# Moving one of four input tiles behind the first weight load, at the start of a fused state-space and dense-layer kernel

## Chip, cores, metric

The kernel runs on one core of a Trainium2 chip. The metric is device time in microseconds (us), median of several executions; lower is better. All times in profiles count from the start of the profiled execution (its span, about 1.4 us shorter than the device time of the same execution). PE is TensorE, PEld its weight loads, DVE is VectorE, ACT is ScalarE, SPq is the queue that issues most DMAs.

## The reference

```python
xn = _layernorm(x)                         # x: 1 x 2048 x 1024, bf16
h  = xn @ w1 + b1                          # w1: 1024 x 3584
dense = (h * tanh(softplus(h))) @ w2       # w2: 3584 x 1024
# state-space part: a diagonal complex recurrence over the 2048 rows of xn
out = x + ssm(xn) + dense
```

This is a condensed form of the reference: the state-space part (two complex projections around the recurrence) plays no role here.

## The kernel before

The kernel works on four blocks of 512 rows. A block is four x tiles of 128 rows (256 KB each). Only the head of the kernel matters here: the first block's x tiles must be loaded, normalized and transposed before TensorE can multiply them with w1. Weights stream through a ring of seven slots of 512 KB. All these loads are issued from one queue, SP, in the order of this code:

```python
    for h in range(2):                      # x tile 0, in two halves
        SP.dma(lambda e, h=h: e.dma_start(xx[:, 0, 0, h * 512:(h + 1) * 512], ...), ...)
    for q in range(1, NQ):                  # x tiles 1, 2, 3
        load_x(SP, 0, q)
    ...                                     # four small loads on the ACT queue
    for i in range(NRING):                  # weights: ring 0 ... ring 6
        ring_load()
        if i == 5:
            SP.dma(... dsk[:] <- A_Dskip.partition_broadcast(P) ...)
```

Who uses what, in program order (cut; `keep_busy(n)` are n dummy matmuls, "fillers", meant to bring TensorE to its faster pace; in the profile of the kernel before, the time from one to the next goes from 107 to 56 ns at about 5.5 us):

```python
    for q in range(2):                      # tiles 0 and 1: statistics on VectorE
        first_sums_v(q, 0); first_sums_v(q, 1); first_var_v(q); first_sqrt(q)
    ...
    first_apply(0);    first_transpose(0)   # normalize on VectorE, transpose on TensorE
    first_apply(1, 2); first_transpose(1)
    keep_busy(8)                            # the last 8 fillers
    first_mean_a(3)                         # tile 3: statistics on ScalarE
    first_copy(0, VE, 0, 4);  first_copy(1, VE, 0, 4)      # lower halves of xnT
    first_copy(0, AC, 4, NK); first_copy(1, AC, 4, NK)     # upper halves, on ScalarE
    ...
    first_sums_v(2, 0); first_sums_v(2, 1)  # tile 2: statistics on VectorE
    ...
    first_apply(2); first_apply(3)
    for f in range(4): first_half(f, 0, 0, NK // 2)        # 16 w1 matmuls: ring 0
    for f in range(4):
        first_half(f, 0, NK // 2, NK)                      # 16 w1 matmuls: ring 1
        if f in (2, 3): first_transpose(f); first_copy(f, VE)
```

So TensorE needs, in this order: tiles 0 and 1, ring 0, ring 1, tile 2, tile 3.

Of the kernel before, what the change touches and what calls it, by code (L numbers as in the profile page):

```python
# [135 lines left out]
def bass_parallel_sum__ssm_conv_s5__dense_activation_mish__prompt_kernel(  # L136
    nc: bass.Bass,
    A_x: bass.AP,
    A_Lambda_re: bass.AP,
    A_Lambda_im: bass.AP,  # L140
    A_B_re: bass.AP,
    A_B_im: bass.AP,
    A_C_re: bass.AP,
    A_C_im: bass.AP,
    A_log_dt: bass.AP,
    A_Dskip: bass.AP,
    B_x: bass.AP,
    B_w1: bass.AP,
    B_b1: bass.AP,
    B_w2: bass.AP,  # L150
    out: bass.AP,
):
    build_kernel(nc, A_x, A_Lambda_re, A_Lambda_im, A_B_re, A_B_im, A_C_re, A_C_im,
                 A_log_dt, A_Dskip, B_w1, B_b1, B_w2, out)


def build_kernel(nc, A_x, A_Lambda_re, A_Lambda_im, A_B_re, A_B_im, A_C_re, A_C_im,
# [7 lines left out]
    NQ = TB // P  # L165
# [13 lines left out]
    SP = Queue(nc, "sp")  # L179
# [104 lines left out]
    def load_x(queue, blk, q):  # L284
        r0 = blk * TB + q * P
        i = blk % 2
        queue.dma(lambda e: e.dma_start(xx[:, i, q, :], A_x[0, r0:r0 + P, :]),  # L287
                  s_xx[i][q] if blk else s_x0[q], writes=[b_xx[i][q]])

    for h in range(2):  # L290
        SP.dma(lambda e, h=h: e.dma_start(xx[:, 0, 0, h * 512:(h + 1) * 512], A_x[0, 0:P, h * 512:(h + 1) * 512]),  # L291
               DmaSem(nc, "d_x00_%d" % h), writes=[b_xx[0][0].parts[h]])
    for q in range(1, NQ):
        load_x(SP, 0, q)
    for src, r0, n in ((A_log_dt, 2 * NJ, NJ), (A_Lambda_im, NJ, NJ), (A_Lambda_re, 0, NJ),
                       (B_b1, 3 * NJ, NF)):
# [9 lines left out]
    def ring_load():  # L306
        i = n_loaded[0]
        if i >= len(items):
            return
        n_loaded[0] += 1  # L310
        kind, g = items[i]
        s = i % NRING
        if kind == "w1":

            dst = ring[:, s, :].rearrange("p (k f) -> p k f", k=NK // 2)
            r0 = (g % 2) * D // 2
            src = B_w1[r0:r0 + D // 2, (g // 2) * 512:(g // 2 + 1) * 512].rearrange("(k p) f -> p k f", p=P)
        else:
            dst = ring[:, s, :].rearrange("p (f d) -> p f d", f=2)
            src = B_w2[g * 256:(g + 1) * 256, :].rearrange("(f p) d -> p f d", p=P)  # L320
        SP.dma(lambda e: e.dma_start(dst, src), s_ring[s], writes=[b_ring[s]])

    for i in range(NRING):
        ring_load()
        if i == 5:
            SP.dma(lambda e: e.dma_start(dsk[:], A_Dskip.partition_broadcast(P)), s_dsk, writes=[b_dsk])

# [571 lines left out]
```

## Time and profile before

| kernel before | |
|---|---|
| median of the first 3 runs | 621.56 us (621.54 to 623.44) |
| span of the profiled execution | 620.4 us |
| TensorE busy | 99% of the span |
| first w1 matmul starts | 9.25 us |
| ring 0 landed | 9.20 us |

Lines of the page of the kernel before: the span; busy time and share of each engine; and the chain of work that ended last, as shares of the span by engine.

```profile
span 620.4 us, 7330 instructions
...
PE 613.6 (99%) x2905; PEld 287.3 (46%) x2961; DVE 462.2 (74%) x677; ACT 247.5 (40%) x161; POOL 50.6 (8%) x47
...
PE 98%; DMA 1%; issue 1%; SPq 0%; DVE 0%
```

TensorE is the limit for 98% of the time. The 1% of DMA is the head. The timeline of the issue queue (start, duration, queue, line, what is loaded, count):

```profile
0.79 0.88 SPq L291 DMA_DIRECT2D xx<-in_A_x_dram  x2
1.72 1.40 SPq L287 DMA_DIRECT2D xx<-in_A_x_dram  x3
3.16 6.28 SPq L321 DMA_DIRECT2D ring<-in_B_w_dram  x6
```

The DMA view of a window that holds only the issue of ring 0 (the last number is the time from issue to landing):

```profile
ring<-in_B_w_dram SPq DMA_DIRECT2D x1, 512.0 KB, 6.0
```

The chain of the first 30 us, in order of time (start, duration, what):

```profile
3.16 6.04 DMA ring<-in_B_w_dram
9.20 0.05 issue
9.25 3.23 PE ps L521 x28
```

Ring 0 is issued at 3.16, lands 6.04 us later, and the first w1 matmuls (line 521) follow at once. The timeline of the same stretch (in brackets: idle time before the group and what ended it):

```profile
8.33 0.61 PE L475 MATMUL ps<-filler 128*128 128x128 bf16 x8
8.74 1.41 DVE L349 BATCH_NORM_STATS2 stats<-xx 128x6 f32<-128x512 bf16 x2
9.24 2.95 PEld L521 LDWEIGHTS ps<-xnT,ring 128*128 128x128 bf16 x28 [0.48 <-DMA ring<-in_B_w_dram]
9.25 3.23 PE L521 MATMUL ps<-xnT,ring 128*128 128x256 bf16 x28 [0.31 <-DMA ring<-in_B_w_dram]
12.21 0.54 PEld L391 LDWEIGHTS ps<-ident,xn 128*128 128x128 bf16 x8
...
18.86 3.23 PEld L663 LDWEIGHTS ps<-xnT,ring 128*128 128x128 bf16 x16
```

The fillers end at 8.94 and TensorE idles 0.31 us for ring 0. VectorE takes tile 2's statistics at 8.74 without waiting. Tile 2's transposes follow at 12.21. The last line is the first weight load of the full-width matmuls, after which no wait of TensorE is listed; it serves below as the mark for the end of the head.

### The profile page before, as it was taken

Reading aid. Unit: us, or ns where it says so; the run is one execution under the profiler, and the core shown is the slowest. Engines: PE = TensorE matmul, PEld = TensorE weight load, DVE = VectorE, ACT = ScalarE, POOL = GpSimd, SP = SyncE. Lnnn points to the kernel's source line nnn. Section 1 sums busy time; section 2 is a strip of 40 time slices with the busy share of each in tenths; the row PEclk is TensorE's granted clock in tenths of the full one; section 3 lists DMA queues with packets and bytes.
Section 4 is the critical chain, followed back from the end, with each engine's and each line's share of the span. In section 5 each row is a group of like instructions: output and inputs, shape, how many; then the busy total and the mean of one; then the engine's idle time right before and its main releaser. Section 6 shows DMA issues by size and latency. Waiting matters only on the chain.

```text
span 620.4 us, 7330 instructions
## 1 busy us (share of the span) xinstructions
PE 613.6 (99%) x2905; PEld 287.3 (46%) x2961; DVE 462.2 (74%) x677; ACT 247.5 (40%) x161; POOL 50.6 (8%) x47
## 2 busy tenths in 40 slices
PE   8999999999999999999999999999999999999998
PEld 7544444444444444444444444444444444444444
DVE  6897899999467599998147759999624856999603
ACT  5689996440069940000008992000001999000000
POOL 1999000000100000000010000000000000000000
DMA  8999965840364300783054430276203541033001
GB/s 286 266 259 260 224 113 189 218 137 0 122 200 153 135 1 36 204 196 109 17 187 136 144 128 1 88 201 172 83 35 104 171 166 68 1 121 117 1 0 69
DMA packets 95804, 79.41 MB, mean 128 GB/s; under 512 B 48922, under 2 KB 78234, under 8 KB 95770
## 3 DMA queue, kind: packets, MB, share of 16 engines
q1 hardware_dynamic: 92272, 71.64, 41.1%
q10 hardware_dynamic: 2538, 4.14, 1.8%
q0 software_dynamic: 960, 3.15, 1.6%
q8 instruction: 24, 0.39, 0.3%
q14 instruction: 10, 0.08, 0.0%
HBM read 63.19 MB, written 4.19 MB: 109 GB/s over the span
## 4 chain that ended last, share of the span: by engine, by line
PE 98%; DMA 1%; issue 1%; SPq 0%; DVE 0%
PE ps L742 49%; PE ps L663 30%; PE ps L684 18%; PE ps L521 1%; DMA ring<-in_B_w_dram 1%; PE ps L756 0%; SPq L287 0%; PE ps L391 0%; SPq L291 0%; DVE xx L810 0%
## 5 line engine op out<-in xcount | busy, mean ns | idle before, releaser
L742 PE MATMUL ps<-ring,act 128*128 128x512 bf16 x880 | 193.2, 379 | 0.8
L663 PE MATMUL ps<-xnT,ring 128*128 128x512 bf16 x840 | 184.4, 379 | 0.8
L642 ACT ACTIVATE act<-hb 128x3584 bf16<-128x3584 bf16 x16 | 50.9, 3183 | 223.5 <-DVE hb L671 223.5
L742 PEld LDWEIGHTS ps<-ring,act 128*128 128x128 bf16 x896 | 87.7, 98 | 105.7
L663 PEld LDWEIGHTS ps<-xnT,ring 128*128 128x128 bf16 x856 | 83.8, 98 | 100.8
L671 DVE TENSOR_SCALAR hb<-ps,par 128x512 bf16<-128x512 f32 x112 | 82.4, 747 | 56.0 <-PE ps L663 54.8
L684 PE MATMUL ps<-xnT,BT 128*128 128x512 bf16 x500 | 110.5, 379 | 0.6
L742 PE MATMUL ps<-CT,hT 128*128 128x512 bf16 x494 | 109.2, 379 | 0.6
L689 DVE TENSOR_TENSOR mt<-ps,tab 128x1024 bf16<-128x1024 f32 x64 | 75.3, 1219 | 17.6 <-PE ps L684 16.6
L684 PEld LDWEIGHTS ps<-xnT,BT 128*128 128x128 bf16 x512 | 50.1, 98 | 60.4
L742 PEld LDWEIGHTS ps<-CT,hT 128*128 128x128 bf16 x506 | 49.5, 98 | 59.7
L707 DVE TENSOR_TENSOR_SCAN hT<-cs,qi,hT 128x512 bf16<-128x512 f32 x48 | 58.9, 1267 | 0.0
L787 DVE TENSOR_TENSOR xx<-ps,xx 128x1024 bf16<-128x1024 f32 (+1 forms) x16 | 18.8, 1189 | 46.1 <-PE ps L742 46.0
L643 ACT ACTIVATE act<-act 128x3584 bf16<-128x3584 bf16 x16 | 51.0, 3190 | 0.2
L644 ACT ACTIVATE act<-act 128x3584 bf16<-128x3584 bf16 x16 | 51.0, 3190 | 0.2
L712 DVE TENSOR_TENSOR mt<-hT,tab 128x1024 bf16<-128x1024 bf16 x64 | 41.4, 688 | 1.1
L649 DVE TENSOR_TENSOR act<-act,hb 128x3584 bf16<-128x3584 bf16 x16 | 32.3, 2016 | 1.3 <-ACT act L644 1.3
L287 POOL DMA_DIRECT2D xx<-in_A_x_dram x12 | 6.7, 559 | 253.2 <-DVE xx L787 247.4
L618 ACT ACTIVATE ct<-CT,cs 128x512 f32<-128x512 bf16 x16 | 11.5, 720 | 26.7 <-DVE CT L620 25.9
L643 ACT ACT_TABLE_LOAD x16 | 20.5, 1283 | 0.3
L644 ACT ACT_TABLE_LOAD x16 | 20.5, 1283 | 0.3
L707 DVE TENSOR_TENSOR_SCAN hT<-cs,hT 128x512 bf16<-128x512 f32 x16 | 18.7, 1208 | 0.0
(86 smaller groups left out, 276.5 us busy)
## 6 DMA issues: line engine op xcount, KB each, us to landing
ring<-in_B_w_dram SPq DMA_DIRECT2D x112, 512.0 KB, 3.9
out_dram<-xx ACTq DMA_DIRECT2D x15, 256.0 KB, 2.1
xx<-in_A_x_dram POOLq DMA_DIRECT2D x12, 256.0 KB, 3.8
xx<-in_A_x_dram SPq DMA_DIRECT2D x3, 256.0 KB, 3.5
xx<-in_A_x_dram SPq DMA_DIRECT2D x2, 128.0 KB, 2.3
dsk<-in_A_Dskip_dram SPq DMA_DIRECT2D x1, 256.0 KB, 8.0
xnT<-xn SPq DMA_TRANSPOSE x12, 4.5
BT<-in_A_B_re_dram SPq DMA_TRANSPOSE x8, 5.8
```

The costliest lines, as they stand in the source:

```text
L642: aop(lambda e: e.activation(a, hs, AF.Exp), reads=[b_hb[g % 2]], writes=[b_act[g]])
L643: aop(lambda e: e.activation(a, a, AF.Ln, bias=1.0), reads=[b_act[g]], writes=[b_act[g]])
L644: aop(lambda e: e.activation(a, a, AF.Tanh), reads=[b_act[g]], writes=[b_act[g]])
L649: vop(lambda e: e.tensor_tensor(a, a, hs, op=ALU.mult), reads=[b_act[g], b_hb[g % 2]], writes=[b_act[g]])
L663: PE.mm(lambda e, k=k, w=w: e.matmul(ps[:, bank, :], lhsT=w, rhs=xnT[:, k, :], start=k == 0, stop=k == NK - 1), reads=[b_ring[s]] + b_xnT, ...
L671: vop(lambda e: e.tensor_scalar(hb[:, hs, :], ps[:, bank, :], b1(f), None, op0=ALU.add), reads=[b_ps[bank], b_par], writes=[b_hbf[hs]])
L684: PE.mm(lambda e, j=j, ci=ci, k=k, bank=bank: e.matmul(ps[:, bank + ci, :], lhsT=BT[:, ci, j, k, :], rhs=xnT[:, k, :], start=k == 0, stop= ...
L689: vop(lambda e, s=s, u=u, j=j: e.tensor_tensor(mt[:, s, :, :], u, tab[:, s, j, :].unsqueeze(1).to_broadcast([P, 2, TB]), op=ALU.mult), rea ...
L707: vop(lambda e, ci=ci, init=init: e.tensor_tensor_scan(out=hT[:, ci, j, :], data0=cj("r", j).to_broadcast([P, TB]), data1=hT[:, ci, j, :], ...
L712: vop(lambda e, s=s: e.tensor_tensor(mt[:, s, :, :], hT[:, :, j, :], tab[:, s, j, :].unsqueeze(1).to_broadcast([P, 2, TB]), op=ALU.mult), ...
L742: PE.mm(lambda e: e.matmul(ps[:, u, :], lhsT=lhsT, rhs=rhs, start=st_, stop=last), reads=reads, writes=[b_ps[u]], first=st_, last=last)
L787: vop(lambda e: e.tensor_tensor(xr, src, xr, op=ALU.add), reads=b_ps[bank:bank + n] + [b_x], writes=[b_x])
```

## The change

The intent: load in the order of use. Tile 2 is wanted after the first weights, so it gives way to them.

```diff
-    for q in range(1, NQ):
+    for q in (1, 3):
         load_x(SP, 0, q)
 ...
     for i in range(NRING):
         ring_load()
+        if i == 0:
+            load_x(SP, 0, 2)
```

## The prediction

> **What bounds the kernel.** TensorE does. The page gives PE 613.6 of 620.4 us (99%), and the chain of waits puts 98% on PE. The waits by engine show no PE wait after 15 us. The change touches only the first 13 us. There PE waits 1.0 us for its first filler, then 0.3 us for a filler behind a VectorE reciprocal, and 0.31 us for the first weights: the fillers end at 8.94 us, the first w1 matmul starts at 9.25. Those 0.31 us, 0.05% of the time, are the whole target.
>
> **The loads before.** The timeline of the DMA-issuing queue: x tile 0 in halves at 0.79 and 1.25, tiles 1, 2, 3 at 1.72, 2.18, 2.67, first weights (ring 0, 512 KB) at 3.16, ring 1 at 3.63. Issue plus time to landing (DMA view of narrow windows): x2 5.7, x3 6.5, ring 0 9.2, ring 1 10.7, ring 2 12.2, ring 3 13.7. Rings land 1.5 us apart, 512 KB at about 350 GB/s: the DMA engines are the limit, not the issue. Landings in the trace come in sixteen parts: 15 of ring 0 by 8.45 us, the last at 9.20. This fits the Trainium skill, "DMA: Bandwidth & Descriptors", section "Queues, rings and completion order": each engine consumes descriptors in ring order, so here order of issue decides order of landing.
>
> **What the change moves.** Nothing is added or removed; x2 (256 KB) goes behind ring 0. At 1.5 us per 512 KB, that is worth 0.75 us (estimate):
> - x3 lands near 5.7 (was 6.5). ScalarE reads it at 6.82: no gain.
> - Ring 0 lands near 8.45 (was 9.20), before the fillers end (8.94); the VectorE copies of xnT end at 8.70. The first w1 matmul starts at about 8.95: up to 0.3 us saved.
> - Ring 1 and later ones have the same bytes ahead and stay at 10.7. PE needs ring 1 after 16 matmuls of 109 ns, 1.75 us: 8.95 + 1.75 = 10.70. The slack of 0.28 us is used up; some 0.05 us can return as a wait there.
> - x2 lands near 9.2 (was 5.7). VectorE took its statistics at 8.74: now about 9.25. Normalized tile 2 ends at 12.0 instead of 11.50, tile 3 at 12.7 instead of 12.23. PE transposed them at 12.21 and 13.09, now would at 11.95 and 12.85: about 0.05 us of wait on tile 2, none on tile 3.
> - Ring 3 (13.7) is wanted at about 13.85: no wait.
>
> So 0.31 us saved, 0.05 to 0.1 given back: net about 0.2 us (0.1 to 0.3), kept to the end since PE is continuous from there. Span 620.4 to about 620.2.
>
> **Predicted time:** 621.3 us, against 621.56. Eight times in ten between 620.3 and 622.3, mostly spread of runs (the three before lie 1.9 us apart). Faster by over 2%: 0.005; within 2%: 0.99; slower by over 2%: 0.005.
>
> **What would show it.** Timeline: first w1 matmul at 8.9 to 9.0, no wait on the ring before it; VectorE's statistics of x2 wait on DMA (about 0.4 us) and start near 9.25; ring 1 still lands near 10.7; the first full-width weight matmul (19.19 before) at about 19.0, everything after 0.2 us earlier.
>
> **What would make it wrong.** If x2 lands after 9.4, the transposes of tile 2 wait for it and the gain vanishes or becomes a loss of a few tenths; if the lagging engine of the sixteen doesn't lose the 0.75 us, ring 0 stays late and nothing is gained. Neither can reach 2%.

## The result

| | before | after |
|---|---|---|
| median, 6 runs each | 621.73 us (621.49 to 623.44) | 621.25 us (621.11 to 622.30) |
| ratio | | 0.999, 95% interval 0.9977 to 1.0003 |
| span of the profiled execution | 620.4 us | 620.0 us |

A ratio is the mean time of one kernel's fast runs over that of the other's of the same rounds, so it is not quite the ratio of the medians quoted. Where the granted clock is listed it is 1.0 for all but two: the slowest run of dsk_first2 (624.82 us) and the slowest of swap_only3 (623.72 us), both at 0.997 and both without a profile.

The page after. The two added lines of code shift all line numbers behind them by two, so L521 is L523 now, L663 is L665.

```profile
span 620.0 us, 7386 instructions
...
PE 616.7 (99%) x2961; PEld 287.2 (46%) x2961; DVE 462.4 (75%) x677; ACT 247.6 (40%) x161; POOL 50.6 (8%) x47
...
PE 99%; DVE 1%; DMA 0%; issue 0%; DVEq 0%
```

PE shows 56 more matmuls and 3.1 us more busy time, though both programs have the same matmuls: the trace before lacks 56 matmul records (2905, with 2961 weight loads). No conclusion may be drawn from that difference. In the chain, 1% has gone from DMA to DVE. The issue queue after:

```profile
1.72 0.92 SPq L287 DMA_DIRECT2D xx<-in_A_x_dram  x2
2.68 0.44 SPq L321 DMA_DIRECT2D ring<-in_B_w_dram  x1
3.16 0.50 SPq L287 DMA_DIRECT2D xx<-in_A_x_dram  x1
3.71 5.60 SPq L321 DMA_DIRECT2D ring<-in_B_w_dram  x5
```

The DMA view of the window with the issue of ring 0:

```profile
ring<-in_B_w_dram SPq DMA_DIRECT2D x1, 512.0 KB, 4.9
```

Issued at 2.68, landed 4.9 us later at 7.6, not at 9.2. The chain after, from its start:

```profile
0.79 2.23 DMA xx<-in_A_x_dram
...
8.38 0.45 PE ps L477 x8
8.82 3.24 PE ps L523 x28
```

Ring 0 is out of the chain: it now runs from the landing of x tile 0 through VectorE and the fillers (L477) into the first w1 matmuls. The timeline:

```profile
8.21 0.61 PE L477 MATMUL ps<-filler 128*128 128x128 bf16 x8
8.70 1.66 PEld L523 LDWEIGHTS ps<-xnT,ring 128*128 128x128 bf16 x16
8.73 3.33 PE L523 MATMUL ps<-xnT,ring 128*128 128x256 bf16 x28
9.05 1.42 DVE L351 BATCH_NORM_STATS2 stats<-xx 128x6 f32<-128x512 bf16 x2 [0.34 <-DMA xx<-in_A_x_dram]
10.57 1.21 PEld L523 LDWEIGHTS ps<-xnT,ring 128*128 128x128 bf16 x12 [0.21 <-DMA ring<-in_B_w_dram]
11.88 0.46 PEld L393 LDWEIGHTS ps<-ident,xn 128*128 128x128 bf16 x8
...
18.45 3.44 PEld L665 LDWEIGHTS ps<-xnT,ring 128*128 128x128 bf16 x17
```

No wait for ring 0; VectorE waits 0.34 us for tile 2; the weight loads now pause 0.21 us for ring 1. The end of the head came 0.41 us earlier (18.45 against 18.86). As a sum: the first w1 weight load came 0.54 us earlier (8.70 against 9.24), and 0.13 us was given back before the mark. The 0.54 are about 0.30 for the wait on ring 0, 0.12 because the fillers ended earlier (8.82 against 8.94), and 0.12 because the weight load, no longer waiting, ran ahead of the fillers' end. The earlier end of the fillers is not the change's doing as far as the order of loads goes: what leads to it is tiles 0 and 1, which were issued as before.

### The profile page after: what moved, and what is told of

Same layout as the page of the kernel before. It is cut to its first block, busy times and chain, and to the rows that moved or that the text cites. A ratio compares the mean times of both kernels' runs of the same rounds, so it can differ in the third digit from the quotient of the medians.

```text
span 620.0 us, 7386 instructions
## 1 busy us (share of the span) xinstructions
PE 616.7 (99%) x2961; PEld 287.2 (46%) x2961; DVE 462.4 (75%) x677; ACT 247.6 (40%) x161; POOL 50.6 (8%) x47
## 4 chain that ended last, share of the span: by engine, by line
PE 99%; DVE 1%; DMA 0%; issue 0%; DVEq 0%
PE ps L744 49%; PE ps L665 30%; PE ps L686 18%; PE ps L523 1%; DVE stats L351 0%; DMA xx<-in_A_x_dram 0%; PE ps L393 0%; PE ps L758 0%; PE ps L477 0%; DVE xx L812 0%; DVE mv L356 0%; DVE rs L377 0%; DVEq L131 0%
## 5 line engine op out<-in xcount | busy, mean ns | idle before, releaser
L665 PE MATMUL ps<-xnT,ring 128*128 128x512 bf16 x856 | 185.4, 379 | 0.0
L665 PEld LDWEIGHTS ps<-xnT,ring 128*128 128x128 bf16 x856 | 83.7, 98 | 100.8
```

Source lines behind the costliest of these rows:

```text
L665: PE.mm(lambda e, k=k, w=w: e.matmul(ps[:, bank, :], lhsT=w, rhs=xnT[:, k, :], start=k == 0, stop=k == NK - 1), reads=[b_ring[s]] + b_xnT, ...
```

## The experiments

Two questions were open. Was the wait of 0.31 us a property of the order of loads (theory A), or of the one execution that was profiled (theory J)? And which part of the change matters? The first submissions of four experiments (null_before, again_after, swap_only, dsk_first) got no chip and gave no result; they were sent again with nearly the same expectations, and these labels end in 2.

The trace records the landing of each load in sixteen parts; a load has landed when its last part has. This table, worked out from those records and the timelines, is the base of most of what follows. "Ready" is the end of the last fillers, "mark" the first full-width weight load, as above.

| profile | ring 0: 15th part | ring 0: last part | ready | first w1 weight load | mark | span |
|---|---|---|---|---|---|---|
| before, first | 8.45 | 9.20 | 8.94 | 9.24 | 18.86 | 620.4 |
| before, second (null_before2) | 8.34 | 8.56 | 8.54 | 8.60 | 18.22 | 619.8 |
| before, third (null_before3) | 8.45 | 8.57 | 8.66 | 8.61 | 18.23 | 619.8 |
| after, first | 7.54 | 7.59 | 8.82 | 8.70 | 18.45 | 620.0 |
| after, second (again_after2) | 7.91 | 7.92 | 8.96 | 8.87 | 18.51 | 620.1 |
| after, third (again_after3) | 7.39 | 8.95 | 8.89 | 8.99 | 19.09 | 620.6 |

In all fourteen profiles, span minus mark is 601.5 to 601.6 us (620.4 - 18.86; 619.8 - 18.22; ...; 622.1 - 20.56 in the slowest). Whatever these fourteen executions differ by was decided before the mark. Where the slower executions without a profile lost their time is not on record.

Medians and means of an experiment are those of 5 runs, set against 9 runs of the kernel before on the same chip.

### The unchanged kernel again: null_before2

No edit.

> A second profile of the unchanged kernel. Theory A (order): ring 0 lands near 9.2 us because x2 is ahead of it, the first w1 matmul starts near 9.25, ratio 1.000. Theory J (jitter): the wait of 0.31 us in the first profile came from one part of sixteen that landed 0.75 us after the others (one packet that took 1.08 us at 5.9 us); here that part can be elsewhere, ring 0 then lands under 8.9 us, there is no wait, and the span is 0.3 us shorter, like that of the changed kernel.

Measured: 621.43 us median (mean 621.81), against 621.24 (mean 621.44) of the same program's other runs; ratio 1.0006 (0.9993 to 1.0018). The chain of the first 30 us, and then the timeline:

```profile
3.14 5.41 DMA ring<-in_B_w_dram
8.56 0.05 issue
8.60 3.23 PE ps L521 x28
```

```profile
7.93 0.61 PE L475 MATMUL ps<-filler 128*128 128x128 bf16 x8
...
8.60 2.95 PEld L521 LDWEIGHTS ps<-xnT,ring 128*128 128x128 bf16 x28 [0.24 <-DMA ring<-in_B_w_dram]
8.60 3.23 PE L521 MATMUL ps<-xnT,ring 128*128 128x256 bf16 x28
```

The same program, with tile 2 ahead of ring 0, took ring 0 in 5.41 us in place of 6.04, TensorE's matmuls lost 0.06 us to it (8.54 to 8.60), and the span was 619.8 us, shorter than any of the three profiles of the changed kernel. The strict theory A is refuted: the 0.31 us are no constant of the program. In the execution that showed them, a single part of the sixteen landed 0.75 us after the others; the trace shows one 1 KB packet of the weights, started at 5.90 us, that took 1.08 us where the median was 0.046 (it does not say to which part that packet belongs).

A part that lagged went on lagging: in that execution the last part came 0.10 us behind the fifteenth for x tile 3, and then 0.75, 0.76, 0.77, 0.78 and 0.74 us behind it for ring 0 to ring 4.

### And once more, on another chip: null_before3

No edit.

> Third profile of the unchanged kernel, and five more times. In all runs so far the span was the start of the first w1 matmul plus 611.1 to 611.2 us plus TensorE's later waits. Theory J2 (the landing of ring 0 varies by up to 1 us from execution to execution and TensorE is exposed to it here): the profile shows ring 0 anywhere from 8.5 to 9.5 us, the span is that plus 611.2, and the five times spread by 1 us or more. Theory A in its strict form (ring 0 near 9.2 each time): profile as the first one, span 620.4, and a spread of 0.3 us.

Measured: 621.84 us median (621.19 to 622.80); the 9 other runs of the same program 621.40; ratio 1.0005 (0.9993 to 1.0018). Ring 0 landed at 8.57, just under the fillers' end; no wait is listed. Theory J2 holds in that ring 0 moves by 0.6 us among three executions of one program and the five times spread by 1.6 us. The two repeated profiles come from different chips (4 and 13), so a part of the 0.6 us may be the chip's; the spread of the five times is from one chip.

### The changed kernel again: again_after2, again_after3

No edit to the changed kernel.

> A second profile of the changed kernel. Theory A: ring 0 lands 7.4 to 8.5 us, first w1 matmul at 8.7 to 8.95 with no wait on the ring, span 0.3 to 0.4 us under that of the unchanged kernel in the same call, ratio 0.9993 to 0.9996. Theory J: no difference from the unchanged kernel beyond 0.1 us on average.

> Third profile of the changed kernel, and five more times. Theory J2: ring 0 lands 7.5 to 8.4 us, ahead of the fillers' end (8.6 to 9.0), so its variation is hidden: no wait on it, the five times lie within 0.4 us of each other at 621.1 to 621.5 (one outlier is not ruled out), below the mean of the unchanged kernel by 0.2 to 0.5 us. Rival (the spread comes from elsewhere): the same spread as the unchanged kernel.

Measured: 621.28 us median (621.17 to 621.47), ratio 0.9998 (0.9985 to 1.0010); and 621.52 (621.18 to 622.08), ratio 0.9998 (0.9984 to 1.0011). The expected ratio of 0.9993 to 0.9996 was not met, the narrow spread was met once (0.3 us) and missed once (0.9 us). The timeline of again_after3 shows why:

```profile
8.99 1.64 PEld L523 LDWEIGHTS ps<-xnT,ring 128*128 128x128 bf16 x16 [0.27 <-DMA ring<-in_B_w_dram]
...
11.20 1.21 PEld L523 LDWEIGHTS ps<-xnT,ring 128*128 128x128 bf16 x12 [0.57 <-DMA ring<-in_B_w_dram]
```

Fifteen parts of ring 0 were there by 7.39, the last came at 8.95: a late part of 1.56 us eats even the larger slack that the new order gives, and ring 1, whose last part was 1.31 us behind its fifteenth, made the weight loads wait again. No packet of the first 12 us of this trace took longer than 0.71 us, so what made the part late is not shown. The timeline of again_after2 shows a cause without any DMA:

```profile
5.21 1.65 PE L477 MATMUL ps<-filler 128*128 128x128 bf16 x14
...
7.41 0.94 PEld L393 LDWEIGHTS ps<-ident,xn 128*128 128x128 bf16 x16
```

These 14 fillers took 1.65 us, 118 ns each; in the first profile of the kernel before they took 1.03 us, 74 ns each. VectorE had finished tile 0 at 6.89, but its transposes started at 7.41, behind the fillers. The Trainium skill, "TensorE: Matmul & The Clock Gate", "Part 1: The HAM clock gate", says that the step from the slow to the fast matmul pace comes about 4 us into sustained activity, "±500ns run-to-run". That the moment varies is seen here too, but by more than the page says: counted from the first filler at 1.04 us, matmuls went from 107 to 56 ns apart after 2.9 us in no_filler, and after more than 5.5 us in again_after2.

### Which bytes ahead of ring 0: dsk_first2

The 256 KB load of the skip vector goes from behind ring 5 to before ring 0, in the kernel before.

```diff
+    SP.dma(... dsk[:] <- A_Dskip.partition_broadcast(P) ...)
     for i in range(NRING):
         ring_load()
-        if i == 5:
-            SP.dma(... dsk[:] <- A_Dskip.partition_broadcast(P) ...)
```

> The 256 KB load of the skip vector moved from behind ring 5 to before ring 0, in the kernel before: 256 KB more ahead of the first weights. Theory A: ring 0 lands near 9.95, first w1 matmul near 10.0, ring 1 near 11.45, time +0.7 us (0.5 to 0.9), ratio 1.0011. Theory J with a slack of 0.5 us in the usual execution: +0.2 to +0.4 us, ratio 1.0005.

Measured: 623.38 us median, ratio 1.0032 (1.0019 to 1.0046), means 623.49 against 621.44: 2.05 us slower, nearly three times the expected 0.7 (1.7 us without the run at a clock of 0.997).

```profile
10.94 3.23 PE L520 MATMUL ps<-xnT,ring 128*128 128x256 bf16 x28 [1.98 <-DMA ring<-in_B_w_dram]
```

Ring 0 landed at 10.90, the first w1 matmul started at 10.94, 2.34 us after that of null_before2, and the span is 2.3 us longer (622.1 against 619.8). That settles one thing: once TensorE waits for ring 0, a microsecond there is a microsecond of the total. It also shows that bytes are not a sufficient measure. The stretch from 6.0 to 9.2 us of this kernel, then of null_before2 (busy time and count by engine, granted clock, DMA share, GB/s):

```profile
6.00:9.20 3.20, 2.96 (x42) 2.49 (x39) 2.87 (x10) 2.47 (x6) 0.00 (x0) 1.00 0.88 236
```

```profile
6.00:9.20 3.20, 3.11 (x43) 2.49 (x41) 3.09 (x11) 2.49 (x6) 0.00 (x0) 1.00 1.04 350
```

With the skip vector in flight the DMA engines moved 236 GB/s, not 350. Its 2 KB packets, all reading one row of memory, took 171 and 267 ns at the median in the two half microseconds from 7.0 to 8.0 (35 of its 128 packets), against 84 ns for those of x. That the shared row is the reason is a guess; the durations are measured.

### The swap without the weights: swap_only2, swap_only3

```diff
-    for q in range(1, NQ):
+    for q in (1, 3, 2):
```

> x tiles in the order 0, 1, 3, 2, all before the weights. Theory A (only what is ahead of ring 0 counts): as the kernel before, ring 0 near 9.2, first w1 matmul near 9.25, ratio 1.000. Rival B (tile 3 earlier helps ScalarE): the gain of 0.3 to 0.4 us is here already, ratio 0.9994.

> The swap of tiles 2 and 3 alone once more, since its five times were 0.6 us over the kernel before on average while its profile showed nothing of the kind. If that was chance: mean within 0.3 us of the unchanged kernel in this call, ratio 1.000. If the swap itself delays ring 0: again 0.4 to 0.8 us over, and the profile shows ring 0 landing after 9.0.

Measured: 622.18 us median, ratio 1.0010 (0.9997 to 1.0022), and 621.89, ratio 1.0009 (0.9996 to 1.0023). Rival B is out: no gain is here. But the mean of the ten runs is 622.08, and that of 28 runs of the unchanged kernel is 621.59. In the profiles ring 0 landed at 8.90 and 9.27. A line of the timeline of swap_only3:

```profile
9.32 3.23 PE L521 MATMUL ps<-xnT,ring 128*128 128x256 bf16 x28 [0.22 <-DMA ring<-in_B_w_dram]
```

The second run met "the swap itself delays ring 0", and I know no reason for it: the same bytes are ahead of ring 0. In that profile the lateness lies in three of the sixteen parts: 13 had landed by 8.35, the others came at 8.90, 9.10 and 9.27. The slowest of the ten runs, 623.72 us, is the one at a clock of 0.997 (0.3% of 622 us is 1.9 us, an estimate from these two numbers); the nine others average 621.90, 0.31 over the unchanged kernel. And two sets of five runs of the unchanged kernel also lay 0.37 and 0.35 us over the nine others of the same program. So 0.5 us on ten runs may be chance or not; this is left open.

### Tile 3 behind ring 0 in place of tile 2: x3_behind

```diff
-    for q in range(1, NQ):
+    for q in (1, 2):
 ...
+        if i == 0:
+            load_x(SP, 0, 3)
```

> x tile 3 goes behind ring 0 in place of tile 2 (order 0, 1, 2, ring 0, 3). If use decides: x3 lands near 9.0; ScalarE's first pass over it, at 6.8 before, waits for it, and ScalarE's copies of the upper halves of xnT stand behind it in program order and end near 11.5, where TensorE wants them at 10.6; tile 3's transposes wait another 0.4 us. Time +1.4 us against the changed kernel, +1.0 us against the kernel before (ratio 1.0016). If it does not matter which tile gives way (rival): as the changed kernel, ratio 0.9994.

Measured: 622.64 us median against 621.45, ratio 1.0017 (1.0004 to 1.0029): the loss is the expected 1.0 us (means 622.64 and 621.64); the waits behind it are only in part the expected ones.

```profile
10.98 1.47 PE L523 MATMUL ps<-xnT,ring 128*128 128x256 bf16 x12 [0.45 <-ACT mv L363]
13.23 0.45 PEld L393 LDWEIGHTS ps<-ident,xn 128*128 128x128 bf16 x8 [1.06 <-DVE xn L381]
```

ScalarE waited for tile 3 until 8.63 and did its copies of the upper halves of xnT after that, ending at 10.83 (9.11 before). The wait of 0.45 us is put down to ScalarE's next instruction (L363), which stands directly behind those copies. The second loss is larger than expected and on tile 2, not 3: its square root stands behind tile 3's second pass in ScalarE's program order. It matters which tile gives way.

### Tile 2 one place further back: x2_behind_two

```diff
-        if i == 0:
+        if i == 1:
             load_x(SP, 0, 2)
```

(an edit of the changed kernel)

> x tile 2 behind ring 1 (order 0, 1, 3, ring 0, ring 1, 2). x2 lands near 10.5; VectorE's statistics of it start there, its normalized tile ends near 13.3, the transposes of tile 2 wait on TensorE for about 1.4 us; the wait on ring 1 is gone. Time +1.3 us against the changed kernel, +0.9 us against the kernel before (ratio 1.0015). Rival (tile 2 has slack beyond ring 0): no loss, ratio 0.9993.

Measured: 622.43 us median against 621.45, ratio 1.0018 (1.0005 to 1.0030), means 622.70 and 621.64: 1.06 us slower.

```profile
9.97 1.42 DVE L351 BATCH_NORM_STATS2 stats<-xx 128x6 f32<-128x512 bf16 x2 [1.55 <-DMA xx<-in_A_x_dram]
12.79 0.45 PEld L393 LDWEIGHTS ps<-ident,xn 128*128 128x128 bf16 x8 [1.41 <-DVE xn L381]
```

Tile 2 landed at 9.95, the weight loads of its transposes waited 1.41 us, and there was no pause at ring 1. Behind ring 0 tile 2 arrives just in time; one place later it is late by more than a microsecond.

### Both tiles behind ring 0: both_behind

```diff
-    for q in range(1, NQ):
+    for q in (1,):
 ...
+        if i == 0:
+            load_x(SP, 0, 3)
+            load_x(SP, 0, 2)
```

> Tiles 3 and 2 both behind ring 0 (order 0, 1, ring 0, 3, 2). Ring 0 lands near 7.0, which buys nothing since TensorE comes to it at 8.8; x3 lands near 8.1, ScalarE waits for it 1.4 us, its copies end near 10.8 against 10.6 wanted, tile 3's transposes wait about 0.3 us. Time +0.5 us against the changed kernel, about +0.1 us against the kernel before (ratio 1.0002). Rival (earlier first weights always help): another 0.3 us gained, ratio 0.999.

Measured: 622.61 us median against 621.45, ratio 1.0018 (1.0004 to 1.0032), means 622.52 and 621.64: 0.9 us slower, where 0.1 was expected. The profiled execution was the fastest of the five (621.70).

```profile
12.16 0.45 PEld L394 LDWEIGHTS ps<-ident,xn 128*128 128x128 bf16 x8 [0.77 <-DVE xn L382]
```

Ring 0 landed at 6.92, far ahead of TensorE's readiness at 8.54, and bought nothing. The wait on the copies didn't appear; tile 2's transposes waited instead, for the same reason as in x3_behind. In the four other executions the loss was larger than the profiled one shows; what they waited for is not on record. The rival "earlier first weights always help" is refuted.

### Without the last fillers: no_filler, no_filler_before

The line `keep_busy(8)` ahead of `first_mean_a(3)` is deleted, in the changed kernel and in the kernel before.

> The changed kernel without the 8 filler matmuls ahead of the first w1 matmul. If ring 1 and tile 2 are the next limits: the first w1 matmul starts near 8.6 in place of 8.8, ring 1 (10.5) then makes TensorE wait about 0.3 us, tile 2's transposes stay at 11.9: no change against the changed kernel (within 0.1 us). Rival (the start of the w1 matmuls is what counts): 0.2 us faster.

> The kernel before without its last 8 fillers, the counterpart of no_filler. TensorE is ready for the weights at about 8.4 to 8.7 us, so the first w1 matmul starts when ring 0 lands (8.5 to 9.3) and removing the fillers gains nothing here: ratio to the kernel before 1.000 within 0.0005, PE's wait on ring 0 grows from 0.0-0.3 to 0.2-0.7 us. Rival (fillers bound the start): 0.2 us faster.

Measured: 621.45 us median, ratio 0.9997 (0.9984 to 1.0009); and 621.86, ratio 1.0004 (0.9992 to 1.0017). no_filler's profile has the first w1 weight load at 8.64, which is no earlier than null_before2's with fillers, then no pause at ring 1, and a span of 619.8. So the expected new wait at ring 1 did not come in this execution, and the small gain that the rival promised can't be told from zero. What came in place of the fillers was a wait for VectorE:

```profile
8.68 3.22 PE L522 MATMUL ps<-xnT,ring 128*128 128x256 bf16 x28 [0.36 <-DVE par L501]
```

The instruction named (L501) stands directly behind VectorE's copies of xnT, which end at 8.53. Without the fillers TensorE idled until VectorE was done, so removing them could not bring the first weights forward by much. In the profile of no_filler_before one part of x tile 1 was late by 0.87 us (15 parts by 4.93, the last at 5.80):

```profile
5.82 1.42 DVE L349 BATCH_NORM_STATS2 stats<-xx 128x6 f32<-128x512 bf16 x2 [1.01 <-DMA xx<-in_A_x_dram]
```

The whole head moved with it and the span was 620.9 us. The wait on ring 0 that had been expected there could not show, because TensorE came too late to need one. No variant tried beats the kernel before clear of noise; no_filler was not timed beside the changed kernel.

### All times together

In the three calls that hold both kernels, the means are 622.04 and 621.42, 621.57 and 621.32, 621.62 and 621.51 us (before, then after; identical programs of a call taken together, 34 and 16 runs in all). The changed kernel is lower each time, by 0.6, 0.2 and 0.1 us. Since sets of runs of one and the same program differed by 0.35 us, a gain of a few tenths is likely but not shown.

## Why the prediction was right

The class (within 2%) and the time (621.25 measured, 621.3 predicted) held. Neither tests the mechanism. Medians of the unchanged program alone lay between 621.24 and 621.84 us, more than the 0.2 us that was forecast, so that the time was met within 0.05 us is luck. Step by step:

- **TensorE bounds all but the head.** Shown: span minus mark is the same within 0.1 us in fourteen profiles, and no wait of TensorE is listed after 15 us in the profile of the kernel before.
- **The order of issue decides the order of landing.** Shown: ring 0 and tile 2 changed places in landing, and in all fourteen profiles the x tiles and the first rings landed in the order in which they were issued. This agrees with the section of the Trainium skill that the prediction names.
- **"Ring 0 lands near 8.45 (was 9.20)".** Wrong by about a microsecond, 7.59. The term of 0.75 us for 256 KB was right: at the fifteenth part, which leaves the late one out, ring 0 landed at 8.41 on average in three profiles before (8.45, 8.34, 8.45) and at 7.61 in three after (7.54, 7.91, 7.39), 0.80 us earlier. Wrong was the number it was taken from: 9.20 held a late part of 0.75 us that belonged to one execution.
- **"Those 0.31 us, 0.05% of the time, are the whole target".** This is the step that failed. It read a wait in one profile as a property of the program. In two more profiles of the same program the matmuls lost 0.06 us and nothing. The change's worth is the average of such waits, which one profile can't give. In the five profiles with all tiles ahead of ring 0 and the fillers in place (three of the kernel before, two of the swap) the matmuls lost 0.31, 0.06, 0, 0.34 and 0.22 us to ring 0, 0.19 on average; in the three of the changed kernel 0, 0 and 0.10.
- **x2 lands near 9.2, statistics near 9.25, a DMA wait of about 0.4 us.** 9.02, 9.05 and 0.34 in the first profile. In the others it landed at 8.59 and 9.68.
- **A small wait at ring 1.** Came as a pause of 0.21 us of the weight loads (0.05 predicted) in the first profile, none in the second, 0.57 in the third.
- **Tile 2's transposes near 11.95.** 11.88, directly behind the normalized tile (11.83); in the second profile that tile was ready 0.3 us ahead. x2_behind_two shows that the next place is too late.
- **Net gain about 0.2 us, span 620.2.** The first pair of profiles shows 0.4 us, but 0.12 of that comes from an earlier end of the fillers, from loads that the change did not move, and other pairs show losses of 0.3 and 0.8 us (619.8 against 620.1 and 620.6). The means over all runs show 0.1 to 0.6.

Why so little: the first w1 matmul waits for the later of two chains, ring 0 and the normalization of tiles 0 and 1. The change moved the first, by its fifteenth part, from 8.4 to 7.6 us on average (its last part came 0.1 to 0.75 us after that before, and 0.01 to 1.56 after the change). The second ends at 8.5 to 9.0 in nearly all profiles, and varies by itself with the landing of tiles 0 and 1 and with the pace of the fillers. So nearly all of the 0.8 us gained on ring 0 is slack, which only a late part can use up.

## What to carry to other kernels

Profile the unchanged kernel two or three times before reading a wait of a few tenths of a microsecond at the head of a kernel as its property. Order loads by first use, but find for each the last moment at which it is still in time: here one place further back for tile 2, or tile 3 in its stead, cost a microsecond. And count what a load costs those behind it by its time in flight, not its bytes: here two loads of 256 KB each cost ring 0 0.8 and 2.3 us.

## What the Trainium skill lacked or had wrong

- "DMA: Bandwidth & Descriptors" has no figure for how the landing of one load varies between executions of a program. Here ring 0 landed at 8.56, 8.57 and 9.20 us in three executions, and the last of sixteen parts came up to 1.67 us behind the fifteenth (x tile 2 in again_after3, 8.01 and 9.68). A lag of 0.75 us stayed through five loads in a row. Its section "Latency and other measured facts" gives an HBM access latency of 0.2 us on average and 2 us at high load; single packets of 1.08 us (median 0.046) and 1.78 us (x tile 2 in the changed kernel, median 0.084) lie below that upper figure, but no run here shows their cause.
- The same page has no figure for a load that broadcasts one row to 128 partitions. Here it used all sixteen parts and still delayed the loads behind it by 2.3 us for 256 KB (packets of 171 to 267 ns against 84), where 256 KB of distinct rows cost 0.80.
- "TensorE: Matmul & The Clock Gate", "Part 1: The HAM clock gate", gives ±500 ns around 4 us for the moment of the clock step; here it came between 2.9 and more than 5.5 us after the first filler. The page does not say that fillers meant to warm the clock can themselves delay the work behind them when the step is late: 14 fillers took 1.03 us in one execution and 1.65 in another, and the transposes then started 0.52 us after their input was ready.
